# Two token-mixing row sums placed in the score banks, one result in the theta buffer, and another order of the last operations

## The chip, the cores and the metric

The kernel runs on one core of a Trainium2 chip. Time is device microseconds of one execution. The runs given are three timed executions of the kernel before (median 200.55 us, from 200.51 to 202.35) and one execution taken with the hardware profiler (201.49 us). Engines are named as the profile names them: PE multiplies matrices, PEld loads its weights, DVE, ACT and POOL do elementwise work, SP issues the loads and stores. PSUM is the memory that PE writes; the kernel sees it as eight banks.

## The reference

Two layers follow each other. The first is a recurrence over 768 tokens for 4 batches of 8 heads of width 40; the second mixes its output over tokens and channels.

```
for t in range(S):
    y[:, :, t] = einsum('bhd,bhde->bhe', rt, state)
    Sa = einsum('bhde,bhe->bhd', state, at)
    state = state * wt - outer(Sa, bt) + outer(vt, kt)
...
theta = x @ w_theta                       # x: y as (4, 768, 320)
zr, zi = x * cos(theta), x * sin(theta)
u = x + (w_tok_r @ zr + w_tok_i @ zi)     # over the 768 tokens of a batch
out = u + max(u @ w_ch, 0)
```

## The kernel before

**Tiles.** The 4 x 768 tokens are 24 tiles of 128 tokens, numbered 0 to 23, six to a batch; tiles 18 to 23 are the last batch. The recurrence is done a tile at a time in matrix form, and the token mixing of a batch starts when its six tiles have their `zr` and `zi`. So after tile 23 the token mixing of the last batch is left, and nothing can be put beside it.

**Order.** Each operation is recorded as an entry with an engine, a function, what it reads and what it writes. Four tables of numbers then decide everything: `ORDER` is the order in which the 1610 entries are issued, `HOMES` the PSUM banks in order of allocation, `PICK` the entries that are done on their second engine, and `WARM` some dummy multiplications at the start. Each engine works through its own queue in that order and waits on semaphores where an entry needs another engine's result. An entry that takes a bank waits until the bank's last reader is done.

**Banks.** Banks 0-1 and 2-3 are two tiles of two banks (`ps_d`), used for the four score products of each recurrence tile; banks 4 to 7 are single (`ps_s`) and hold everything else.

**Names.** These entries are met in what follows; a number behind a name is the tile.

| entry | engine | what it does |
|---|---|---|
| `slv`, `slu` | PE | scores in half-height mode (64 rows), into a two-bank tile, line 536 |
| `mlv`, `mlu` | DVE, or ACT with a later `sel` on POOL | causal mask while copying the scores out: lines 546, 548, 550 |
| `nut`, `gd`, `xt`, `ut` | PE | transposes; `enut`, `egd`, `ext`, `eut` copy them out, on ACT or DVE (lines 380, 383, 643) |
| `y`, then `ex` | PE, DVE | output of the recurrence (722 to 731), scaled into x (738) |
| `th`, `thj` | PE | theta; for two tiles at a time the last part is a pair of half-height products, `thj` (692, 702) |
| `eth`, `cos`, `sin` | ACT | theta copied to the buffer `th` (757), then its cosine and sine (772, 777) |
| `zr`, `zi` | POOL, or DVE | x times cosine and sine (792, 791) |
| `row18.3` | PE | two multiplications of 128x320: the share of tile 18+3 in tile 18's token mixing (805). The six of a tile accumulate in one bank |
| `uadd` | DVE | that sum plus x, 812 |
| `ch`, `chj` | PE | channel product, with a half-height pair `chj` for two tiles at once (692, 702); tiles 22 and 23 are done alone, with three products each |
| `oo`, then `st` | DVE, SP | result into one of three buffers `oo_t[t % 3]` (828), store of 160 KB (831) |

Of the kernel before, what the change touches and what calls it, by code (L numbers as in the profile page):

```python
# [12 lines left out]
ALU = mybir.AluOpType  # L13
# [8 lines left out]
RUNS = 8  # L22
ORDER = [
# [185 lines left out]
def kernel(  # L209
# [14 lines left out]
    nc = tc.nc  # L224
# [743 lines left out]
```

## Time and profile before

| | us |
|---|---|
| median of three timed runs | 200.55 |
| the profiled execution | 201.49 |
| its span, first to last instruction | 199.8 |
| PE busy | 190.1 (95%) |
| DVE, ACT, POOL busy | 165.5 (83%), 158.1 (79%), 144.6 (72%) |
| store `out_dram<-oo`, issue to landing, min / median / max | 1.8 / 1.9 / 5.2 |

Times in the profile count from the first instruction. A row of the timeline or of the chain is: start, duration, engine, line, operation, result and operands, count, and in brackets how long the engine stood idle before it and what ended that. Multiplications are pipelined, so one row's duration runs into the next row; what an entry costs PE is the distance from its first row to the next entry's first row. The granted TensorE clock is 1.00 through the whole span.

### The profile page before, as it was taken

What the parts mean: (1) busy time and instruction counts of PE and PEld (TensorE: products, weight loads), DVE (VectorE), ACT (ScalarE), POOL (GpSimd) and SP (SyncE); (2) the same over time, 40 slices, a digit from 0 to 9 for tenths busy, and PEclk for the clock granted to TensorE, in tenths of its full rate; (3) what the DMA queues carried; (4) which work ended last, traced back from release to release, by engine and by line L of the source; (5) the groups of instructions that cost most, each with busy time, mean ns of one, the idle gap of its engine ahead of it and who ended that gap; (6) DMA issues with size and microseconds to landing.
All of it is one profiled execution on the core that took longest, in us unless ns stands there. A gap on an engine that the chain in (4) does not pass through costs nothing.

```text
span 199.8 us, 8121 instructions
## 1 busy us (share of the span) xinstructions
PE 190.1 (95%) x3354; PEld 153.3 (77%) x3354; DVE 165.5 (83%) x261; ACT 158.1 (79%) x347; POOL 144.6 (72%) x209
## 2 busy tenths in 40 slices
PE   7888999997999999999999999999999999999992
PEld 6776787875887788878787978887888768776761
DVE  5378899999999898987897999999999976478342
ACT  3686889999999989699986898889998957695001
POOL 8286465586998999699799767887697665369200
PEclk9999999999999999999999999999999999999999
DMA  6999888899999899999989999988848240100222
GB/s 128 219 180 199 168 170 175 177 177 197 208 178 190 157 198 190 225 192 201 185 194 174 201 198 192 191 184 155 164 71 185 59 127 3 66 3 34 102 98 98
DMA packets 127365, 31.03 MB, mean 155 GB/s; under 512 B 117664, under 2 KB 127328, under 8 KB 127328
## 3 DMA queue, kind: packets, MB, share of 16 engines
q1 hardware_dynamic: 124544, 27.54, 68.6%
q0 software_dynamic: 2784, 2.97, 9.6%
q8 instruction: 26, 0.43, 0.9%
q14 instruction: 11, 0.09, 0.1%
HBM read 29.54 MB, written 3.93 MB: 168 GB/s over the span
## 4 chain that ended last, share of the span: by engine, by line
PE 67%; SPq 8%; DMA 7%; ACT 5%; POOL 4%; DVE 4%; issue 3%; POOLq 0%; DVEq 0%; ACTq 0%
PE ps_s L805 17%; PE ps_s L377 12%; PE ps_d L536 9%; PE ps_s L692 6%; SPq L394 5%; PE ps_s L660 3%; SPq L406 3%; DMA raw_r<-in_r_dram 3%; PE ps_s L508 2%; DMA raw_kb<-in_k_dram 2%; PE ps_s L616 2%; PE ps_s L702 2%; PE ps_s L595 2%; DMA raw_v<-in_v_dram 2%; PE ps_s L879 2%
## 5 line engine op out<-in xcount | busy, mean ns | idle before, releaser
L414 POOL TENSOR_TENSOR kb<-raw_kb,ex 128x320 bf16<-128x320 f32 x46 | 36.8, 812 | 6.4 <-ACT ex L447 2.5
L805 PE MATMUL ps_s<-zr,wtok_r 128*128 128x320 bf16 x144 | 40.9, 299 | 0.1
L805 PE MATMUL ps_s<-zi,wtok_i 128*128 128x320 bf16 x144 | 40.8, 299 | 0.0
L546 DVE TENSOR_TENSOR psi<-ps_d,mask_p 128x1024 bf16<-128x1024 f32 x22 | 26.8, 1218 | 1.2 <-PE ps_d L536 1.1
L546 DVE TENSOR_TENSOR lamu<-ps_d,mask_p 128x1024 bf16<-128x1024 f32 x22 | 26.8, 1216 | 0.5 <-PE ps_d L536 0.5
L546 DVE TENSOR_TENSOR phi<-ps_d,mask_n 128x1024 bf16<-128x1024 f32 x19 | 23.1, 1218 | 1.4 <-PE ps_d L536 1.4
L414 POOL TENSOR_TENSOR ah<-raw_a,we 128x320 bf16<-128x320 f32 x22 | 19.0, 866 | 4.7 <-DMA raw_a<-in_a_dram 2.4
L546 DVE TENSOR_TENSOR lamv<-ps_d,mask_p 128x1024 bf16<-128x1024 f32 x16 | 19.5, 1219 | 2.7 <-PE ps_d L536 2.4
L792 POOL TENSOR_TENSOR zi<-cs,xp 128x320 bf16<-128x320 f32 x22 | 17.4, 805 | 4.2 <-ACT cs L777 4.2
L792 POOL TENSOR_TENSOR zr<-cs,xp 128x320 bf16<-128x320 f32 x20 | 16.2, 819 | 2.6 <-ACT cs L777 2.6
L631 POOL TENSOR_TENSOR gt<-sum,ex 128x320 bf16<-128x320 f32 x13 | 9.6, 736 | 10.8 <-DVE sum L627 7.9
L805 PEld LDWEIGHTS <-wtok_r 128*128 128x128 bf16 x144 | 14.0, 97 | 4.3
L536 PE MATMUL ps_d<-aT,kbT 64*128 64x128 bf16 x384 | 16.7, 217 | 0.5 <-ACT kbT L380 0.5
L805 PEld LDWEIGHTS <-wtok_i 128*128 128x128 bf16 x144 | 14.0, 97 | 3.6 <-issue 0.3
L377 PE MATMUL ps_s<-wide,kb 128*128 128x128 bf16 x192 | 15.2, 223 | 0.4 <-POOL kb L414 0.4
L512 ACT COPY rT<-ps_s 128x512 bf16<-128x512 bf16 x24 | 13.3, 593 | 2.3 <-PE ps_s L508 2.2
L812 DVE TENSOR_TENSOR up<-ps_s,xp 128x320 bf16<-128x320 f32 x22 | 10.7, 488 | 5.1 <-PE ps_s L805 4.8
L729 PE MATMUL ps_s<-kb,lamv 128*128 128x40 bf16 x192 | 14.7, 180 | 0.0
L731 PE MATMUL ps_s<-kb,lamu 128*128 128x40 bf16 x192 | 14.6, 179 | 0.0
L536 PEld LDWEIGHTS <-kbT 64*128 64x128 bf16 x384 | 11.6, 94 | 3.8 <-ACT kbT L380 1.6
L380 ACT COPY uT<-ps_s 128x320 f32<-128x320 f32 (+1 forms) x11 | 4.6, 414 | 12.3 <-PE ps_s L660 12.2
L729 PEld LDWEIGHTS <-lamv 128*128 128x128 bf16 x192 | 13.2, 96 | 0.5
(164 smaller groups left out, 618.5 us busy)
## 6 DMA issues: line engine op xcount, KB each, us to landing
raw_w<-in_w_dram SPq DMA_DIRECT2D x24, 160.0 KB, 4.0
raw_v<-in_v_dram SPq DMA_DIRECT2D x24, 160.0 KB, 3.9
raw_a<-in_a_dram SPq DMA_DIRECT2D x24, 160.0 KB, 4.0
raw_kb<-in_k_dram SPq DMA_DIRECT2D x24, 160.0 KB, 3.9
raw_kb<-in_b_dram SPq DMA_DIRECT2D x24, 160.0 KB, 4.2
raw_r<-in_r_dram SPq DMA_DIRECT2D x24, 160.0 KB, 4.1
out_dram<-oo SPq DMA_DIRECT2D x24, 160.0 KB, 1.9
wrow_i<-in_moe_w_tok_i_dram POOLq DMA_DIRECT2D x6, 192.0 KB, 4.6
```

Source lines behind the costliest of these rows:

```text
L377: nc.tensor.transpose(out=dst[:, c:c + 128], in_=pair(src, g), identity=ident)
L394: lambda dst=dst, src=src: nc.sync.dma_start(out=dst, in_=src),
L414: pool = ("POOL", lambda: nc.gpsimd.tensor_tensor(out=dst, in0=in0, in1=in1, op=ALU.mult))
L512: add("ACT", "e" + nm, i + x, lambda x=x, dst=dst: nc.scalar.copy(out=dst.rearrange("p (g t q) -> p g t q", g=G, q=8), in_=ps(pr).bitcast( ...
L536: nc.tensor.matmul(t[:, q, g, :], lhsT=lhs[rows(q), g * 128:(g + 1) * 128], rhs=rhs[rows(q), g * 128:(g + 1) * 128], start=True, stop=True)
L546: add("DVE", kindm, i, lambda: nc.vector.tensor_tensor(out=flat, in0=whole(), in1=mask.to_broadcast([128, 2 * G, 128]), op=ALU.mult), 1217 ...
L692: nc.tensor.matmul(ps(pk)[:, 0:DM], lhsT=lhs[:, c * n + kt, :], rhs=wt[:, 3 * c + kt, :], start=kt == 0, stop=kt == 2, skip_group_check=n ...
L729: nc.tensor.matmul(o, lhsT=lamv[:, p, g, :], rhs=kb[:, 0, h, 0:D], start=first, stop=False, skip_group_check=True)
L731: nc.tensor.matmul(o, lhsT=lamu[:, p, g, :], rhs=kb[:, 1, h, 0:D], start=False, stop=True, skip_group_check=True)
L792: pool = ("POOL", lambda: nc.gpsimd.tensor_tensor(out=dst, in0=in0, in1=in1, op=ALU.mult))
L805: nc.tensor.matmul(ps(pk)[:, 0:DM], lhsT=wtok[nm][j][:, s], rhs=zs[c][:, s], start=n == 0 and c == 0, stop=n == NT - 1 and c == 1)
L812: add("DVE", "uadd", q, lambda: nc.vector.tensor_tensor(out=u, in0=ps(pk)[:, 0:DM], in1=x, op=ALU.add), 488, [pk, x_key(q)], [u_key(q)], a ...
```

## The change

`row` sums of tiles 22 and 23 take a two-bank tile of the scores and use its first half; the result of tile 20 (N - 4) goes into the last slice of the theta buffer instead of `oo_t[2]`; `ORDER`, `HOMES` and `PICK` are new.

```diff
+LAST = (22, 23)
...
     def mix_row(bi, j):
         q = bi * NCH + j
-        pk = ("ps", "row", q)
+        pk, wide_home = ("ps", "row", q), q in LAST
+
+        def acc():
+            return ps(pk)[:, 0, 0:DM] if wide_home else ps(pk)[:, 0:DM]
...
-                    nc.tensor.matmul(ps(pk)[:, 0:DM],
-                                     lhsT=wtok[nm][j][:, s],
+                    nc.tensor.matmul(acc(), lhsT=wtok[nm][j][:, s],
...
-                new=(pk, 1) if n == 0 else None, tail=tail(320))
+                new=(pk, 2 if wide_home else 1) if n == 0 else None, tail=tail(320))
         add("DVE", "uadd", q, lambda: nc.vector.tensor_tensor(
-            out=u, in0=ps(pk)[:, 0:DM], in1=x, op=ALU.add), 488,
+            out=u, in0=acc(), in1=x, op=ALU.add), 488,
...
-            ck, u, oo = ("ps", "ch", t), u_of(t), oo_t[t % 3]
+            ck, u = ("ps", "ch", t), u_of(t)
+            oo = th_t[0][:, NT - 1] if t == N - 4 else oo_t[t % 3]
+            ok = ("th", NT - 1) if t == N - 4 else ("oo", t % 3)
```

Most of the numbers in the order table stand elsewhere than before, but entries of different engines only pass each other there: engine by engine, the built programs have the same instructions in the same order up to `y21` on PE, `oo13` on DVE, `mlv22` on ACT, `wgt22` on POOL and `st12` on SP (a few waits sit on a neighbouring instruction, through banks that swap places). Behind these the queues are, before:

```
PE    x023 row16.0 row16.1 xt20 nu23 row16.2 gd22 row16.3 th21 nut23 th20 thj20 slu22 slu23 row17.0
      ut14 row17.1 row17.2 row17.3 row17.4 row17.5 y22 y23 row16.4 xt22 row16.5 ch14 xt23 ch15 chj14
      ut16 th22 th23 ch16 ch17 chj16 row19.0 row19.1 row21.0 row18.0 row18.1 row18.2 row19.2 row18.3
      row21.1 row19.3 row21.2 row18.4 row19.4 row18.5 row21.3 row19.5 row20.0 row20.1 row20.2 ut18
      row21.4 row21.5 row20.3 row20.4 row20.5 ch18 ch19 chj18 ut20 row22.0 row22.1 row22.2 ch20 ch21
      chj20 row22.3 row22.4 row23.0 row23.1 row23.2 row22.5 row23.3 row23.4 row23.5 ut22 ut23 ch22 ch23
DVE   ex21 ext20 enut23 mlu22 eut14 uadd17 ex22 ex23 ext22 uadd16 oo15 oo14 zr19 oo16 zr22 zi22 oo17
      uadd18 uadd19 uadd21 uadd20 oo19 oo18 oo20 uadd22 oo21 uadd23 oo22 oo23
ACT   enut22 nx23 mlv23 enu23 egd22 eth20 mlu23 eth21 cos21 cos18-20 sin21 sin18-20 ext23 eut16 eth22
      sin23 cos23 cos22 sin22 eut18 eut20 eut22 eut23
POOL  sel23 sel22 sel23 zr20 zi21 zi18 zr18 zi19 zi20 zr21 zr23 zi23
SP    st13 st14 st17 st16 st15 st19 st18 st20 st21 st22 st23
```

and after:

```
PE    row16.0 x023 row16.1 row16.2 xt20 nu23 ut14 row16.3 row16.4 nut23 row16.5 ch15 ch14 th20 th21
      chj14 thj20 slu22 slu23 gd22 row17.0 row17.1 row17.2 row17.3 row17.4 row17.5 y22 y23 ut16 xt22
      row22.0 row23.0 xt23 th22 ch17 ch16 chj16 th23 row22.1 row18.0 row21.0 row18.1 row21.1 row19.0
      row18.2 row20.0 row19.1 row19.2 row19.3 row18.3 row18.4 row19.4 row19.5 row18.5 row20.1 row21.2
      row20.2 row20.3 ut18 row20.4 row20.5 row21.3 ch18 ch19 chj18 row22.2 row21.4 row22.3 row22.4
      row21.5 row23.1 row23.2 row23.3 row22.5 ut20 row23.4 row23.5 ut22 ch20 ch21 chj20 ut23 ch22 ch23
DVE   enut22 ex21 mlv23 eut14 uadd16 oo14 mlu22 mlu23 uadd17 ex22 ex23 eut16 ext23 oo15 oo17 oo16 zi20
      zr22 zr23 uadd19 uadd18 oo19 oo18 uadd20 uadd21 uadd22 uadd23 oo20 oo21 oo22 oo23
ACT   nx23 ext20 enu23 enut23 eth20 eth21 sin18-20 egd22 cos18-20 sin21 ext22 cos21 eth22 cos23 sin23
      cos22 sin22 eut18 eut20 eut22 eut23
POOL  sel22 zi18 zr18 zi19 zr19 zr20 zr21 zi21 zi23 zi22
SP    st14 st13 st16 st17 st15 st18 st19 st20 st21 st22 st23
```

More of the change, by code (lines that the diff above doesn't have):

```diff
@@ L829, in channels @@
                 out=oo, in0=ps(ck)[:, 0:DM], scalar=0.0, in1=u, op0=ALU.max,
-                op1=ALU.add), 488, [ck, u_key(t)], [("oo", t % 3)], at="row")
+                op1=ALU.add), 488, [ck, u_key(t)], [ok], at="row")
             add("SP", "st", t, lambda bi=bi, j=j, oo=oo: nc.sync.dma_start(
-                out=out_r[bi, j], in_=oo), 350, [("oo", t % 3)], [], at="row", work=550)
+                out=out_r[bi, j], in_=oo), 350, [ok], [], at="row", work=550)
     def mixer_weights():
```

222 rows, old and new, of tables (HOMES, ORDER, PICK) are left out of this document.

## Prediction

> **What bounds the kernel now.** The page comes first: PE is busy 190.1 of 199.8 us, and its slices are full until the last. So only what PE waits for, and what follows its last work, can move the end. As the queues differ only behind 171 us, I read the chain of waits from 180 us on, which names those places:
>
> ```profile
> 183.06 1.01 POOL zr L792
> 184.07 0.04 issue
> 184.11 3.42 PE ps_s L805 x24
> ...
> 193.69 0.02 issue
> 193.72 0.04 DVE us L812
> 193.75 0.37 issue
> 194.12 0.48 DVE oo L828
> 194.60 0.43 DVE us L812
> 195.03 0.05 issue
> 195.08 0.36 PE ps_s L660 x3
> ...
> 196.55 0.49 DVE oo L828
> ```
>
> The chain leaves PE twice before its end: for a `zr` (row18.3 starts at 184.11) and for `uadd23` (`ut23` starts at 195.08). Then come `ut23`, its copy, `ch23`, `oo23` and a store. The timeline of PE gives the size of both waits and of a third cost:
>
> ```profile
> 174.43 0.31 PE L702 MATMUL ps_s<-wth,xT 64*128 64x320 bf16 x2
> 174.58 0.63 PE L536 MATMUL ps_d<-rT,nuT 64*128 64x128 bf16 x16
> ...
> 179.30 0.43 PE L692 MATMUL ps_s<-wch,uT 128*128 128x320 bf16 x2
> 179.67 0.31 PE L702 MATMUL ps_s<-wch,uT 64*128 64x320 bf16 x2
> 179.91 0.45 PE L660 MATMUL ps_s<-wide,up 128*128 128x128 bf16 x5
> ```
>
> A half-height pair followed by half-height work costs PE 0.15 (174.43 to 174.58). Between full-height work it costs 0.24 (179.67 to 179.91), and the `ch15` ahead of it 0.37 (179.30 to 179.67) where two 128x320 products otherwise take 0.27. So going in and out costs 0.19 together.
>
> **What the change removes.** PE's work behind 171.44 is the same, entry for entry; up to `ut23` it is everything but `ch22` and `ch23`. Three items can go.
>
> The wait for `uadd23`: `ut22` starts at 194.33 and costs 0.16, as `xt22` does (178.43 to 178.59), so PE stands from 194.49 to 195.08, 0.59. After the change `ut22`, `ch20`, `ch21`, `chj20` stand between `row23.5` and `ut23`: 0.27 for `row23.5` itself, then 0.16 + 0.27 + 0.37 + 0.24 = 1.31 in all. `uadd23` needs 1.02 from `row23.5`'s start (194.06 to its end, 195.02, and 0.06 to PE). Covered by 0.3. The same holds for tile 22, whose cover is 1.10, and for `ut20`'s copy, 0.99 against 0.96: thin, and worth at most 0.1 each.
>
> The wait for `zr21`: row18.2 of 183.31, row19.2 of 183.58, then row18.3 at 184.11 instead of 183.85, 0.26.
>
> The mode pair: `chj14` moves next to `thj20` and `slu22`, 0.19.
>
> Together 1.04, so `ut23` would start at 195.08 - 1.04 = 194.04, if no new wait comes.
>
> **Where new waits could come.** I go through the after queues with PE's costs by kind, starting from 171.44: `thj20` then ends at 176.05 and `slu23` at 176.5; `y23` starts at 178.89, row22.0 at 179.89, row18.4 at 185.55, row19.5 at 186.09.
>
> Masks. The masks of `lamv23` and `lamu23` leave ACT (1.03 and 1.02) and POOL (a select of 1.09 each) for DVE (line 546: 1.22 each, 1.15 start to start). DVE has room: between 170 and 175 us it is busy 2.29 of 5. But `mlu22` and `mlu23` now run in series behind `oo14`, which waits for `chj14` (end 175.90). `oo14` starts at 175.94, `mlu22` at 176.36, `mlu23` at 177.51 and ends at 178.73, 0.05 to PE: `y23` at 178.89 finds it ready, by 0.11. Costed at nothing; every tenth that DVE is later is a tenth of PE. `enut22` to DVE, `enut23` and `ext20` to ACT, `eut16` and `ext23` to DVE trade copies of 0.3 to 0.5 between engines that stand idle around them: nothing.
>
> POOL's products. Before, three selects are queued there ahead of the products; now one. ACT copies both thetas (from 176.08), takes the sine of three tiles from 176.86 (0.45 after the second copy, as 176.17 to 176.62 before), copies `gd22` out, and ends the cosine at 179.0. `zr18` needs it, so POOL starts it about 179.1 and ends about 179.9, when row22.0 is due: up to 0.1 late. From there POOL makes one product each 0.75. What DVE does beside it costs extra, in both timelines:
>
> ```profile
> 183.02 1.04 POOL L792 TENSOR_TENSOR zr<-cs,xp 128x320 bf16<-128x320 f32 x1
> 184.02 1.04 POOL L792 TENSOR_TENSOR zr<-cs,xs 128x320 bf16<-128x320 f32 x1
> 185.02 0.79 POOL L792 TENSOR_TENSOR zi<-cs,xs 128x320 bf16<-128x320 f32 x1
> ```
>
> A POOL product takes 0.79, and 1.04 behind a DVE product; DVE's, issued at 183.33, ends at 184.41, 0.35 after the POOL product under way. After the change DVE makes three (`zi20`, `zr22`, `zr23`), POOL nine. With one to three of POOL's lengthened by 0.25, `zi22` ends between 185.5 and 185.95, and row18.4 at 185.55 waits 0 to 0.45. `zr23` ends about 185.9, before row19.5 at 186.09. I take 0.2 for all of POOL.
>
> **The end.** `ut23`, copy, `ch23`, `oo23` stay as they are, 1.47 from `ut23` to the start of `oo23` (195.08 to 196.55). What differs is the stores. Before, three of the last four are spread over 4 us; after, `oo20` to `oo23` start 0.1, 0.5, 0.9 and 1.5 behind `ut23`, and the stores follow. DMA activity in 40 slices, for one store alone (180 to 184 us), then for three issued at 184.84, 185.22 and 185.70 (184 to 188 us):
>
> ```profile
> DMA  0000000000000000028989400000000000000000
> ```
>
> ```profile
> DMA  0000000000000000289997989979998400000000
> ```
>
> One starts 0.8 after its issue at 180.94 and moves for 0.6; three in a row take 1.55, 0.52 each. Four from `ut23` + 1.50 on end at + 3.6 (0.52 each) to + 3.9 (0.6 each), where the last alone, as before, ends at + 3.42. So the queue costs 0.15 to 0.45; I take 0.2, as stacked stores are the nearer row. By the Trainium skill ("DMA: Bandwidth & Descriptors", Anatomy of one DMA) the part of a transfer that grows with its size is bytes/436e3 us, an estimate of 0.38 for 160 KB; stores 0.4 apart would then not queue and the sum would be 0.2 better. That fit is for another issuing path, and the rows here say 0.52.
>
> `oo20` in the theta buffer costs what any `oo` costs (486 ns). It keeps `oo23` from waiting for tile 20's store, which it would meet: that store is issued at `ut23` + 0.66 and lands 1.9 later, + 2.56, while `oo23` starts at + 1.47. Before, the distance was 4 us. So: nothing, as written. The score banks are free for `row22.0` and `row23.0` when `mlu22` and `mlu23` have read them (178.73, against 179.89): nothing. `st14` ahead of `st13` and the like on SP: nothing waits for these stores.
>
> **Sum.** -1.04 + 0.2 + 0.2 = -0.64 on the profiled execution: 201.49 to 200.85. That execution is 0.94 above the median of the runs, its span 1.73 below its own time; the difference is taken off the median: 200.55 - 0.64 = 199.9. Ends of the terms: -1.04 + 0 + 0.15 = -0.9 and -1.04 + 0.45 + 0.45 = -0.15, so 199.65 to 200.4 by these alone.
>
> **Rivals.**
> 1. *Products in time, stores free.* If no product comes late and stores do not queue, all of 1.04 stays: 199.5. For it: stacked stores overlap already. Against: `oo` come every 0.41, a store takes 0.52.
> 2. *Given back.* row18.4 waits 0.45, the stores queue for 0.45, thin covers cost 0.15: 1.04 - 1.05, 200.55. For it: covers of 0.03 to 0.1 at `ch20`, `ut22` and row22.0. Against: needs all together. It is also what one sees if the order does not do what it says.
> 3. *Slower, by the masks.* `y23` waits for `mlu23`. Above 0.8 of delay the gain is gone, as stores still cost 0.2. One mask behind (1.15 - 0.11 = 1.04 of waiting) relieves POOL's 0.2 and gives -1.04 + 1.04 + 0.2 = +0.2: 200.75; two would give 201.9. For it: two masks now follow each other on DVE, one of which had ACT and POOL. Against: the 0.11 is with everything else on time, and DVE idles 0.9 ahead of `oo14`.
>
> Chances: the sum 0.52, rival 1 0.18, rival 2 0.20, rival 3 0.10. The three runs spread by 1.8 us, mostly through one, and a median can move by some tenths. Range 199.3 to 200.8. About 1% (2 us) is what a measurement here tells from no change. No case reaches that to the fast side, since all waits of PE behind 171 us and the mode pair are 1.04; the slow side needs more than two masks' delay. What is left on either side is for what the queues don't show: faster 0.03, same 0.92, slower 0.05.
>
> **What would show it.** Right: `ut23` near 194.2 in the span, with no wait ahead of it; one half-height block less; `zi22` ending within 0.4 of row18.4; the last four stores without a gap in DMA activity, ending 3.6 behind `ut23`. Wrong: a wait of PE at `y23` or at a `row` of more than 0.5, `oo23` waiting for a store, or a difference ahead of 171 us, where the queues are the same.

## The result, and the profile after

| | before | after |
|---|---|---|
| median of 20 timed runs, us | 200.94 (200.03 to 203.26) | 200.05 (199.33 to 202.97) |
| ratio, 95% interval | | 0.994 (0.9914 to 0.9966) |
| the profiled execution, us | 201.49 | 199.71 |
| its span, us | 199.8 | 198.0 |

By the ratio the change is worth 1.2 us (0.7 to 1.7), by the medians 0.89; the forecast was 0.64, a ratio of 199.9 / 200.55 = 0.9968, just above the interval. That is no change at the bound of 1%, as forecast, though the interval ends below 1, and the predicted time of 199.9 is 0.15 off.

The span is 1.8 shorter in the profiled executions, more than anything forecast. To see where, I cut each span at two places that every kernel has: the start of `y21` on PE, up to which the queues of both kernels hold the same, and the start of `ut23`.

| stretch, us | before | after | difference |
|---|---|---|---|
| first instruction to `y21` | 170.89 | 170.05 | -0.84 |
| `y21` to `ut23` | 24.19 | 23.15 | -1.04 |
| `ut23` to the last store's last packet | 3.44 | 3.53 | +0.09 |

The rows on which the second stretch rests, `y21` and `ut23` in PE's timeline, before and after:

```profile
170.89 0.20 PE L722 MATMUL ps_s<-gd,rT 128*128 128x80 bf16 x1
...
195.08 0.34 PE L660 MATMUL ps_s<-wide,us 128*128 128x128 bf16 x3 [0.42 <-DVE us L812]
```

```profile
170.05 0.20 PE L723 MATMUL ps_s<-gd,rT 128*128 128x80 bf16 x1
...
193.20 0.34 PE L661 MATMUL ps_s<-wide,us 128*128 128x128 bf16 x3
```

The second stretch is shorter by exactly the 1.04 of the three removed items, with no new wait against it. The chain of waits of the changed kernel (start, duration, what), from 181.88 on:

```profile
181.88 5.18 PE ps_s L809 x38
187.06 0.28 PE ps_s L661 x5
...
192.31 0.17 PE ps_s L661 x3
192.48 0.54 PE ps_s L693 x4
193.02 0.24 PE ps_s L703 x2
193.27 0.29 PE ps_s L661 x3
...
193.63 0.33 ACT uT L381
...
194.01 0.58 PE ps_s L693 x3
...
194.68 0.49 DVE oo L833
```

Before, this chain left PE for a `zr` at 183.06 and for `uadd23` (`us L812`) at 194.60. Now L809 (the `row` sums) runs through, and between the transposes of tiles 22 (192.31) and 23 (193.27) stand `ch20`, `ch21` and `chj20` (lines 693 and 703). (The chain puts such a row up to 0.16 later than the timeline: 193.27 here and 193.20 above are the same `ut23`.) Only then does the chain leave PE, for `ut23`'s copy. That exit is the old one.

The mode pair in PE's timeline after: `chj14`, `thj20` and `slu22` follow each other at 0.14 and 0.14, one half-height block where there were two.

```profile
174.75 0.31 PE L703 MATMUL ps_s<-wch,uT 64*128 64x320 bf16 x2
174.89 0.30 PE L703 MATMUL ps_s<-wth,xT 64*128 64x320 bf16 x2
175.03 0.61 PE L537 MATMUL ps_d<-rT,nuT 64*128 64x128 bf16 x16
```

The two thin places of the forecast, in the timelines of DVE and POOL after:

```profile
175.50 2.35 DVE L547 TENSOR_TENSOR lamu<-ps_d,mask_p 128x1024 bf16<-128x1024 f32 x2
```

```profile
178.13 0.79 POOL L793 TENSOR_TENSOR zr<-cs,xp 128x320 bf16<-128x320 f32 x1 [0.37 <-ACT cs L778]
...
182.64 2.04 POOL L793 TENSOR_TENSOR zi<-cs,xs 128x320 bf16<-128x320 f32 x2
```

The two masks end at 175.50 + 2.35 = 177.85, and `y23` starts at 178.03: ready by 0.18, of which 0.05 is the way to PE. `zr18` ends at 178.92 for `row22.0` at 179.03. The last product, `zi22`, ends at 182.64 + 2.04 = 184.68. `row18.4` starts at 184.72 and needs `zi22` only for its second multiplication, at 184.86: 0.18 early.

DMA activity in 40 slices of 0.1 us, first before (195 to 199 us), then after (194 to 198 us):

```profile
DMA  0000289994000000000000289895059988100000
```

```profile
DMA  0000002999879998799987999820000000000000
```

Before, the last two stores are two blocks; after, the last four are one, from 194.65 to 196.73, 2.08 or 0.52 each. That block ends 3.53 behind `ut23`, instead of 3.44.

### The profile page after: what moved, and what is told of

It is laid out like the page before. It is cut to its first block, busy times and chain, and to the rows that moved or that the text cites. A ratio compares the mean times of both kernels' runs of the same rounds, so it can differ in the third digit from the quotient of the medians.

```text
span 198.0 us, 8123 instructions
## 1 busy us (share of the span) xinstructions
PE 189.6 (96%) x3354; PEld 153.8 (78%) x3354; DVE 167.6 (85%) x263; ACT 156.2 (79%) x345; POOL 142.3 (72%) x207
## 4 chain that ended last, share of the span: by engine, by line
PE 71%; ACT 10%; SPq 6%; DVE 5%; issue 4%; DMA 2%; POOL 0%; DVEq 0%; ACTq 0%
PE ps_s L809 16%; PE ps_s L378 12%; PE ps_d L537 9%; PE ps_s L693 6%; SPq L395 4%; PE ps_s L661 4%; PE ps_s L617 3%; PE ps_s L509 3%; DMA raw_kb<-in_k_dram 2%; PE ps_s L703 2%; PE ps_s L596 2%; SPq L407 2%; PE ps_s L732 2%; PE ps_s L884 2%; PE ps_d L809 2%
## 5 line engine op out<-in xcount | busy, mean ns | idle before, releaser
L809 PE MATMUL ps_s<-zr,wtok_r 128*128 128x320 bf16 x132 | 37.5, 299 | 0.0
L809 PE MATMUL ps_s<-zi,wtok_i 128*128 128x320 bf16 x132 | 37.5, 299 | 0.0
L547 DVE TENSOR_TENSOR lamu<-ps_d,mask_p 128x1024 bf16<-128x1024 f32 x23 | 27.9, 1216 | 0.3 <-PE ps_d L537 0.3
L793 POOL TENSOR_TENSOR zi<-cs,xp 128x320 bf16<-128x320 f32 x21 | 16.4, 793 | 9.2 <-ACT cs L778 9.2
L547 DVE TENSOR_TENSOR lamv<-ps_d,mask_p 128x1024 bf16<-128x1024 f32 x17 | 20.7, 1219 | 2.6 <-PE ps_d L537 2.4
L809 PEld LDWEIGHTS <-wtok_r 128*128 128x128 bf16 x144 | 14.0, 97 | 4.1
L809 PEld LDWEIGHTS <-wtok_i 128*128 128x128 bf16 x144 | 14.0, 97 | 3.4
L833 DVE SCALAR_TENSOR_TENSOR oo<-ps_s,up 128x320 f32<-128x320 f32 x21 | 9.5, 486 | 5.1 <-PE ps_s L703 4.2
L378 PEld LDWEIGHTS <-kb 128*128 128x128 bf16 x192 | 12.0, 100 | 1.4 <-POOL kb L415 0.6
```

Source lines behind the costliest of these rows:

```text
L378: nc.tensor.transpose(out=dst[:, c:c + 128], in_=pair(src, g), identity=ident)
L547: add("DVE", kindm, i, lambda: nc.vector.tensor_tensor(out=flat, in0=whole(), in1=mask.to_broadcast([128, 2 * G, 128]), op=ALU.mult), 1217 ...
L793: pool = ("POOL", lambda: nc.gpsimd.tensor_tensor(out=dst, in0=in0, in1=in1, op=ALU.mult))
L809: nc.tensor.matmul(acc(), lhsT=wtok[nm][j][:, s], rhs=zs[c][:, s], start=n == 0 and c == 0, stop=n == NT - 1 and c == 1)
L833: add("DVE", "oo", t, lambda ck=ck, u=u, oo=oo: nc.vector.scalar_tensor_tensor(out=oo, in0=ps(ck)[:, 0:DM], scalar=0.0, in1=u, op0=ALU.max ...
```

## The experiments

Timed ratios separate few of these kernels, since an effect of 0.2 to 1 us stands against intervals of 0.3 to 0.6% (0.6 to 1.1 us) to either side. So each is judged by the cut of its own profile, in which PE's granted clock is 1.00 behind 170 us in every case. Ahead of 170 us it is not: `before_again`, `after_again` and `e3_ch20_early` had 0.93 over their first 25 us, `e4_rows_late` from 75 to 100 us. All are edits of the changed kernel unless the text says otherwise; ratios are to the kernel before. The sum is from `y21` to the last packet.

| kernel | `y21` to `ut23` | `ut23` to `oo23` | `ut23` to last packet | sum | ratio (95%) |
|---|---|---|---|---|---|
| before | 24.19 | 1.47 | 3.44 | 27.63 | |
| after | 23.15 | 1.48 | 3.53 | 26.68 | 0.994 (0.9914 to 0.9966) |
| before_again | 24.18 | 1.47 | 3.43 | 27.61 | 0.9998 (0.9963 to 1.0033) |
| after_again | 23.14 | 1.48 | 3.53 | 26.67 | 0.9972 (0.9939 to 1.0006) |
| e6_old_head | 23.14 | 1.48 | 3.54 | 26.68 | 0.9929 (0.9897 to 0.996) |
| e1_oo20_back | 23.14 | 2.55 | 4.49 | 27.63 | 0.9999 (0.9965 to 1.0033) |
| e3_ch20_early | 23.93 | 1.47 | 3.41 | 27.34 | 0.9965 (0.9915 to 1.0015) |
| e2_chj14_alone | 23.31 | 1.48 | 3.53 | 26.84 | 0.9971 (0.9919 to 1.0024) |
| e7_zi20_pool | 23.76 | 1.49 | 3.55 | 27.31 | 0.9987 (0.9934 to 1.0041) |
| e5_mlu23_act | 24.14 | 1.48 | 3.52 | 27.66 | 0.9986 (0.9952 to 1.0019) |
| e4_rows_late | 23.95 | 1.48 | 3.52 | 27.47 | 1.0029 (0.9973 to 1.0084) |

**Is the stretch ahead of `y21` faster too?** Both kernels were run once more (`before_again`, `after_again`), and a kernel with the changed queues behind `y21`, but with the order and the banks of before ahead of it (`e6_old_head`).

```diff
-ORDER, HOMES: as in the changed kernel
+ORDER, HOMES: those of before up to y21 on PE (and the like on the other engines), then the changed ones
```

> The kernel before once more. Theory (the head varies by chance): y21 to ut23 is 24.19 within 0.05, and y21 starts up to 1 us away from 170.89. Rival (the head is slower in this kernel): y21 starts within 0.2 of 170.89.

> The changed kernel once more, as the measure for the others. Theory: y21 starts anywhere from 169.5 to 171.5 us, y21 to ut23 is 23.15 within 0.05, 0.9 us faster than the kernel before. Rival (the head is faster too): y21 starts near 170.05 again, 1.5 us faster or more.

> The changed kernel with the issue table and the banks of the kernel before for everything ahead of the point where the queues differ; behind it the changed queues (the banks renamed to fit). Theory (the 0.83 by which the changed kernel's profile is ahead at y21 is chance, and its gain is that of the last 30 us, 0.95): y21 to ut23 23.15, time level with the changed kernel, 0.9 under the kernel before. Rival (the other banks and waits ahead of 171 us are worth 0.8 themselves): 0.8 slower than the changed kernel, about level with the kernel before.

The distances behind `y21` come back to 0.01. The kernel with the old head stands level with the changed one: the order and the banks ahead of the divergence make no difference that shows. And the start of `y21` moves by itself: 170.05, 170.44, 170.69, 171.29 and 172.34 in the changed kernel, e1, e5, e2 and e7, whose queues ahead of it are the same and whose clock was 1.00 over the first 50 us. They are not all from one chip: e1 and e2 share one, and these two alone are 0.85 apart; e7 ran on another, where the kernel before takes 202.53 in the median against 201.62 on theirs. The 0.84 of the profiled pair lies inside that spread. The two repeated runs settle less than they were made for. `before_again` starts `y21` at 170.89 once more, which theory and rival both allow. `after_again` starts it at 173.25, outside the 169.5 to 171.5 that were expected, and its clock of 0.93 over the first 25 us doesn't explain that alone, since `before_again` had the same.

In the profiled pair a lead shows early: the same cast of `r`, a row of POOL's timeline, before and after:

```profile
49.48 0.72 POOL L420 CAST r<-raw_r 128x640 bf16<-128x640 f32 x1 [1.37 <-DMA raw_r<-in_r_dram]
```

```profile
47.40 0.72 POOL L421 CAST r<-raw_r 128x640 bf16<-128x640 f32 x1
```

Before, POOL stood idle for 1.37 until the load had landed; after, the load was there. What made it earlier wasn't traced.

**The result in the theta buffer** (`e1_oo20_back`). Tile 20's result goes back to its own buffer.

```diff
-            oo = th_t[0][:, NT - 1] if t == N - 4 else oo_t[t % 3]
-            ok = ("th", NT - 1) if t == N - 4 else ("oo", t % 3)
+            oo, ok = oo_t[t % 3], ("oo", t % 3)
```

> The changed kernel with one edit: tile 20's result in oo_t[2] again. Theory (the theta buffer only spares oo23 the wait for tile 20's store): PE as in the changed kernel, 23.15 us from the start of y21 to the start of ut23; oo23 stands until tile 20's store has landed, about 1.0 us later than the 1.48 behind ut23 that it has in the changed kernel, so that the last store's packets end about 0.9 later (its queueing of 0.1 goes): 0.9 us slower than the changed kernel, about level with the kernel before. Rival (the buffer is free in time, the theta buffer buys nothing): no wait ahead of oo23, time as the changed kernel.

`ut23` keeps its place, but the timeline of DVE shows `oo23` (last row) idle 1.16 until a store has landed:

```profile
194.49 0.48 DVE L832 SCALAR_TENSOR_TENSOR oo<-ps_s,us 128x320 f32<-128x320 f32 x1
196.13 0.49 DVE L832 SCALAR_TENSOR_TENSOR oo<-ps_s,us 128x320 f32<-128x320 f32 x1 [1.16 <-DMA out_dram<-oo]
```

It starts 2.55 behind `ut23` instead of 1.48, and the end moves by 0.96: the whole gain is gone (sum 27.63, as before). The forecast had put the meeting at + 2.56.

**The work between the last two transposes** (`e3_ch20_early`). `ut20` with its copy, `ch20`, `ch21` and `chj20` move up to their neighbours among the last sums.

```diff
 PE  ... row23.3
-    row22.5 ut20 row23.4 row23.5 ut22 ch20 ch21 chj20 ut23 ch22 ch23
+    ut20 row22.5 row23.4 ch20 ch21 chj20 row23.5 ut22 ut23 ch22 ch23
```

> The changed kernel with the last entries of PE reordered so that ch20, ch21 and chj20 no longer stand between row23.5 and ut23: ut20 goes ahead of row22.5, and ch20 ch21 chj20 ahead of row23.5. Theory (they are the cover of uadd23): ut23 waits for uadd23 as before the change, 0.6 us, and ch20 for ut20's copy 0.1; y21 to ut23 grows from 23.15 to about 23.85, the end by 0.6, as the stores of tiles 20 and 21 start earlier. Rival (DVE's and the stores' chain behind chj20 sets the end, so that earlier ch20 and ch21 pull it in): end within 0.1 of the changed kernel's or earlier, though ut23 is later.

PE's timeline:

```profile
195.70 0.30 PE L809 MATMUL ps_d<-zr,wtok_r 128*128 128x320 bf16 x1
195.84 0.30 PE L809 MATMUL ps_d<-zi,wtok_i 128*128 128x320 bf16 x1
196.11 0.72 PE L693 MATMUL ps_s<-wch,uT 128*128 128x320 bf16 x4
...
197.29 0.33 PE L661 MATMUL ps_s<-wide,us 128*128 128x128 bf16 x3
198.08 0.33 PE L661 MATMUL ps_s<-wide,us 128*128 128x128 bf16 x3 [0.46 <-ACT uT L381]
```

From `ut22` (197.29) to `ut23` (198.08) it is 0.79, where 0.17 is its cost and 0.75 stood before: the old wait of 0.6 is back. (The bracket names ACT's copy; `uadd23` ends at 197.49 + 0.49 = 197.98 on DVE and is what `ut23` transposes.) `row23.4` to `ch20` takes 0.41 instead of 0.27, 0.14 of waiting for `ut20`'s copy, whose cover is gone too. The stores get 0.12 back, as `oo20` and `oo21` come earlier.

**The mode pair** (`e2_chj14_alone`). `chj14` moves back to just behind `ch14`, away from `thj20`.

```diff
-    ch15 ch14 th20 th21 chj14 thj20 slu22 slu23
+    ch15 ch14 chj14 th20 th21 thj20 slu22 slu23
```

> The changed kernel with one entry moved on PE: chj14 right behind ch14, among full-height work, instead of next to thj20. Theory (a half-height block costs PE 0.19 for going in and out): y21 to ut23 grows from 23.15 to 23.34, time +0.2. Rival (PE hides the switch, as oo14 and the masks behind it can start 0.9 earlier): no change within 0.05.

```profile
175.44 0.31 PE L703 MATMUL ps_s<-wch,uT 64*128 64x320 bf16 x2
175.68 0.72 PE L693 MATMUL ps_s<-wth,xT 128*128 128x320 bf16 x4
176.33 0.31 PE L703 MATMUL ps_s<-wth,xT 64*128 64x320 bf16 x2
176.48 0.61 PE L537 MATMUL ps_d<-rT,nuT 64*128 64x128 bf16 x16
```

In PE's timeline `chj14` costs 0.24 (175.44 to 175.68) when full-height work follows, against 0.14 after. `ut23` comes 0.16 later.

**Where the products are made** (`e7_zi20_pool`). `zi20` goes back to POOL, behind `zr20`.

```diff
-DVE   ... oo16 zi20 zr22 zr23        POOL  ... zr20 zr21 zi21 zi23 zi22
+DVE   ... oo16 zr22 zr23             POOL  ... zr20 zi20 zr21 zi21 zi23 zi22
```

> The changed kernel with one product, zi20, on POOL behind zr20 instead of on DVE. Theory (POOL's chain of products is what row18.4 is due on; a DVE product lengthens the next POOL product by 0.25, since DVE works off its product after the POOL product under way): POOL has a product more, 0.75, and still two of 1.04, so zi22 ends 0.75 later and row18.4 waits about 0.75; y21 to ut23 grows from 23.15 to 23.9. Rival 1 (a DVE product costs POOL as much as it saves): POOL ends within 0.3, y21 to ut23 at most 23.45. Rival 2 (PE has slack there): 23.15.

PE's timeline at `row18.4`, and POOL's last products:

```profile
187.00 0.30 PE L809 MATMUL ps_s<-zr,wtok_r 128*128 128x320 bf16 x1
187.76 0.30 PE L809 MATMUL ps_s<-zi,wtok_i 128*128 128x320 bf16 x1 [0.46 <-POOL zi L793]
```

```profile
185.67 2.04 POOL L793 TENSOR_TENSOR zi<-cs,xs 128x320 bf16<-128x320 f32 x2
```

One product more makes `zi22` end at 187.71, 15.37 behind `y21` instead of 14.63: 0.74 later. `row18.4`'s first multiplication starts on time; its second, due at 187.14, waits until 187.76. That is 0.62 of the 0.75 expected: the rest is the slack of `zi22`, which the trace after puts at 0.13 (184.86 - 184.68, less 0.05 to PE). This row shows that a product can be late by one multiplication without cost, which the forecast had not counted.

**Where the mask is made** (`e5_mlu23_act`). `mlu23` goes back to ACT, with its select on POOL.

```diff
-DVE   ... mlu22 mlu23        ACT  ... eth20 eth21            POOL  sel22 zi18 zr18
+DVE   ... mlu22              ACT  ... eth20 mlu23 eth21      POOL  sel22 sel23 zi18 zr18
```

> The changed kernel with the mask of lamu23 done as before the change: copied out by ACT (between the two copies of theta) and masked by a select on POOL. Theory (on DVE it costs nothing, on ACT and POOL it delays the products): sines and products come about 1.0 later, so PE waits at row22.0 for zr18 or at row18.4 for zi22; y21 to ut23 grows from 23.15 to about 24.0, +0.9. Rival (it does not matter where the mask is made): within 0.1 of 23.15.

PE's timeline at `y22` and at `row22.0`, and ACT's:

```profile
178.79 0.20 PE L723 MATMUL ps_s<-gd,rT 128*128 128x80 bf16 x1 [0.51 <-ACT gd L644]
...
180.66 0.30 PE L809 MATMUL ps_d<-zr,wtok_r 128*128 128x320 bf16 x1 [0.17 <-POOL zr L793]
```

```profile
176.32 1.02 ACT L549 ACTIVATE lamu<-ps_d 128x1024 bf16<-128x1024 f32 x1
177.24 0.42 ACT L758 COPY th<-ps_s 128x320 f32<-128x320 f32 x1
177.55 1.02 ACT L778 ACTIVATE cs<-th 128x960 f32<-128x960 f32 x1
178.45 0.29 ACT L644 COPY gd<-ps_s 128x160 f32<-128x160 f32 x1
```

The 1.02 of the mask on ACT pushes everything behind it: the copy of `gd22` ends at 178.74, and `y22`, which reads it, starts 0.94 behind `row17.5` instead of 0.27. Then `row22.0` waits 0.33 more, for `zr18`. Together 1.0, where 0.9 was expected, and the larger part is the copy and not a product. So the masks on DVE aren't an idle trade of engines in this order: with one of them on ACT the gain of the removed waits is lost.

**The rows that are put early** (`e4_rows_late`). `row22.0`, `row23.0` and `row22.1` move to just ahead of `row22.2`.

```diff
-    xt22 row22.0 row23.0 xt23 th22 ... th23 row22.1 row18.0 ... chj18 row22.2
+    xt22 xt23 th22 ... th23 row18.0 ... chj18 row22.0 row23.0 row22.1 row22.2
```

> The changed kernel with row22.0, row23.0 and row22.1 moved on PE from 179 to 181.5 us to just ahead of row22.2 (189 us); the banks stay. Theory (the score banks let PE do 0.81 us of work while the products are still being made; POOL's last product for row18.4, ending 0.04 before it is due, fixes that point): row18.4 starts where it started, 14.7 behind y21, after waits that sum to 0.8, and y21 to ut23 grows from 23.15 to about 23.95: +0.8. Rival (products come in time anyway, the banks buy nothing): no waits, y21 to ut23 stays at 23.15.

The size was right and the place wrong. `row18.4` starts 14.66 behind `y21`, as after, although 0.81 of work was taken from ahead of it, and that work then comes on top. But PE doesn't stand at `row18.4`. The chain of waits:

```profile
183.43 0.97 DVE xs L739 x2
184.40 0.41 DVE uT L384
...
184.85 0.58 PE ps_s L693 x3
...
185.45 0.43 ACT th L758
...
186.30 0.50 DVE oo L833
...
186.85 0.72 PE ps_s L809 x4
```

It waits at `xt23` (starts 184.46, 0.47 behind `xt22`) for `ex23`, the second L739 product, which ends at 184.40; at `th22` (184.85) for the copy that ends at 184.81; and at `row18.0` (186.85) for an `oo` that ends at 186.80. What the early rows do is fill these places. Without these waits the products would still have held PE close by: `zi22` ends at 189.83 here, and `row18.4`'s second multiplication starts at 189.98.

## Why the prediction was right, and by how much it was off

**What the change removes** held to the hundredth: 1.04 forecast, 1.04 measured (24.19 to 23.15). The parts are off by some hundredths that cancel, so the exact fit is partly luck. Where an experiment took them singly, the mode pair is 0.16, forecast 0.19, and the wait for `uadd23` 0.6, forecast 0.59, back in e3. The wait for `zr21` (forecast 0.26) wasn't undone by itself; 1.04 - 0.6 - 0.16 leaves 0.28 for it.

**The products** were mis-sized: 0.2 taken, nothing measured. Two steps of that term failed. `zi22` came at the early end of the range given for it (0.04 ahead of `row18.4`'s start, forecast 0.05 ahead to 0.4 behind). Two of POOL's products show 1.04, the middle of the "one to three" assumed, which with the forecast's start of the chain would have put it 0.1 behind. It came earlier because the chain started earlier: ACT's sine starts 0.32 behind the second copy of theta (175.55 to 175.87), where 0.45 was taken from before, and `zr18` ends 0.11 ahead of `row22.0`, where it was forecast to end when the row is due. And a row's first multiplication needs only its `zr`, so the true need is 0.14 later than the forecast had it.

**The stores** were over-sized too: 0.2 taken, 0.09 measured (3.44 to 3.53). The 0.52 each of stacked stores, taken from three in a row, is what four showed; the first began to move at + 1.45 instead of + 1.50, and the end was to be + 3.6 and is + 3.53. So the 0.09 lies just below the 0.15 to 0.45 given. By the Trainium skill ("DMA: Bandwidth & Descriptors", Anatomy of one DMA), whose fit is for another issuing path, the stores would not have queued (0.38 each, an estimate). The trace after has one unbroken block and disagrees. The Trainium skill ("DMA: Bandwidth & Descriptors", Where 436 GB/s comes from) puts the limit of one core between HBM and SBUF at about 358 GB/s, which makes 0.46 for 160 KB, an estimate. That is nearer to the measured 0.52.

**Masks** at nothing: right, with 0.13 of cover at `y23` where 0.11 was forecast. **`oo20`** at nothing, and + 2.56 without the theta buffer: right (2.55 in e1). **The score banks** at nothing: no new wait shows at `row22.0` or `row23.0`. Whether those rows could start as early from other banks wasn't tried.

So behind `y21` the change is worth 1.04 - 0.09 = 0.95, against 0.64 forecast, a ratio of about 0.9953 that lies in all three intervals of the kernels with the changed end (after, after_again, e6). That the time itself came within 0.15 is luck: the gain was forecast 0.31 too small, and the median from which it was taken, 200.55, lies 0.39 below that of 20 runs, 200.94. The gain can't be shared out among the experiments either: undone one at a time, the six edits of the last 30 us cost 0.16 to 0.98 each and 4.2 together, so each shows only that its part is needed in this order.

**Rivals.** The first (products in time, stores free) was half right: the products are in time, the stores aren't free. The second (given back) and the third (masks) did not occur, but their mechanisms are real and close: e7 shows a late product, and one mask elsewhere gives 0.99 back. The third in its own form, DVE late at `y23`, wasn't provoked.

**A difference ahead of `y21`**, which the forecast named as a sign that it was wrong, did come, and is 0.84 of the profiled 1.8. The spread of `y21` and e6 speak for chance. It should have been named as noise of the profiled execution, to be taken off before the sum is compared.

## What to carry to other kernels

Ahead of a drain that nothing can cover, keep a little work of other tiles whose inputs are ready, and put it between the last producer and its consumer: 0.88 us of it (`ch20`, `ch21`, `chj20`) hid a wait of 0.6 here. Before you count work on the busiest engine as saved because it goes elsewhere, ask what the engine waits for next: taking 0.81 from ahead of a late input moved nothing forward. And compare two profiled executions stretch by stretch from a common event, since a stretch that is the same in both, here the one ahead of `y21`, may move by more than the change is worth.

## What the runs showed of the hardware

The start of `y21` moved by 2.3 us (170.05 to 172.34) between profiled executions whose queues ahead of it were the same and whose granted clock was 1.00 (on more than one chip; 0.85 between two on the same chip), while every distance behind it, where few loads are left, came back to 0.01. In the pair above the same cast starts 2.08 us earlier where its load had landed in time; 0.84 of lead is left at `y21`.

A product of two SBUF operands on DVE (`zi20`, 182.00) beside one on POOL (`zi21`, 181.89 to 182.68) took 1.03 and ended 0.35 after it, and POOL's next, issued at 182.64, took 1.04 instead of 0.79:

```profile
182.00 1.03 DVE L792 TENSOR_TENSOR zi<-cs,xp 128x320 bf16<-128x320 f32 x1
```

```profile
181.89 0.79 POOL L793 TENSOR_TENSOR zi<-cs,xp 128x320 bf16<-128x320 f32 x1
```

All 43 products that DVE makes in the eleven profiles end 0.35 after the POOL product beside which they were issued (0.346 to 0.353), and only POOL products behind one of them take 1.03 to 1.05. After the change `zr23` runs beside POOL's last product and so lengthens none. So the product moved from POOL to DVE freed POOL for 0.74 (e7), and cost DVE twice the 0.49 of an `oo`.
